# Attention, experts and a squared-ReLU layer on one core: the units of a step in another order

## The chip, the cores and the metric

One core of one Trainium2 chip runs the whole program in one launch. The metric is the device time in microseconds (us); before the change it is 1945.49 us, the median of 3 runs (1945.02 to 1945.93).

## The reference

Three parts follow one another; everything is float32.

```python
# 1. attention: 4 batches, 8 heads, 576 positions, head size 64
scores = q @ k.T / 8        # heads 0-3: the last 32 positions
                            # heads 4-7: every 4th of the last 128
x = softmax(scores) @ v     # -> x [2304, 512]
# 2. experts: 8 experts of width 1024, all of them for every token
P = exp(x @ w_gate - max)   # then 8 rounds that scale rows and columns
out = sum_e P[:, e] * (relu(x @ w1[e]) @ w2[e])
# 3. a dense layer of width 2048
y = relu(out @ w_in) ** 2 @ w_out
```

## The kernel before, in words

After the attention the kernel runs 80 steps. Steps 0 to 31 take the 8 experts in quarters of 256 hidden columns for tokens 0 to 1023 (and a single block of 256 tokens, 1024 to 1279); steps 32 to 63 (32 is `NS1`) take the same weights for tokens 1280 to 2303; steps 64 to 71 and 72 to 79 are the dense layer for the two pairs of token blocks. `first` holds 0, 32, 64, 72; `TURN` is 4, `SCALED` 3.

Every float32 number is split into a high part, rounded to the type that TensorE multiplies, and a low part, and a product is three: high by high, high by low, low by high. Each layer multiplies 2 x 2 blocks with seven products in place of eight (Winograd's form), so the operands are sums and differences of blocks, and results are built up in PSUM banks, copied to another bank as a common part, and added to.

In layer one the seven units of step i are u1 to u7 (`l1_pair`), six products of 512 columns each, 1.36 us. They use three banks, tiles s, pt, xt: bank_a (u1, u3), bank_b (a copy of u1's result, then u4, u5, u6) and bank_c (u2, u7). After u4 ScalarE copies bank_b to s2 (L771), after u5 to s3 (L775); VectorE adds bank_c to s3 (L776), and only then may u7 overwrite bank_c; after u7 it adds bank_c to s2 (L787). L723 takes the ReLU of a result times the token's gate as r1 (u3), r2 (u5), r3 (u6), r4 (u7).

Layer two of step i - 1 runs in step i, where a step is "mixed" (5 to 64 and 73 to 79). Its units are v1m to v7m for output half m = 0, 1 (`l2_mixed`, line 946), three products each, 0.68 us: a half unit. Their left operands are made from r1 to r4: GpSimd forms the differences (L736, "mix", and L734, r3 - r5), ScalarE casts the high part (L702), VectorE subtracts the low part (L705). Operand 11 comes from u3, 22 from u5, 21 from u6, t1 to t4 from the mix after u7. v1 uses 11, v2 uses 21, v3 22, v4 t4, v5 t1, v6 t2, v7 t3. Each chain of units shares banks: v6, v3 and then v7, v4 add to one bank that VectorE (L957) has to read in between; half 0 ends its chain in bank x, half 1 in bank z, so v41 may write z only after the add of v71 has read it. "cp" is a ScalarE copy into half 1's second bank; that bank is bank_a, so cp waits until L723 has read r1 from it. In steps 0 to 31 there are also us (layer one of the single block, 24 products of 256 columns, L806), w0 and w1 (its layer two, six products each, L849), and the weights of the next step are split: a high part on ScalarE (L174) and a low part on VectorE (L178), with sums of blocks on GpSimd (L192 to L197, L246 to L251). In steps 32 to 63 the split weights are fetched from DRAM.

The order is written by hand. `names` lists a mixed step's units; a + joins units into one slot. `run` issues a unit and then what is due in its slot; `after(k, f)` puts f into the k-th slot from now. Every engine works through its own instructions in the order issued, and the SyncE queue (SP) issues all transfers in order. So the list sets both TensorE's order and, by the counts k, that of the other four. In a step of 5 to 30 the list has 17 slots; the parts of the next weights fall in fixed slots (`prep_w`).

Other work rides along: `split_on` splits activation blocks for later steps (a cast, then a low part, two stores and a GpSimd subtraction), and `narrow_on` turns int64 words of the dense layer's weights (they hold float64) into float32 in pieces of three VectorE stages each; `work` gives the slots of the stages, `loads` those of a piece's load. Three pieces (`DEEP`) were done in steps 3 and 4, the rest from step 33. `turn` (line 916) transposes the single block's sums in step 32.

Of the kernel before, what the change touches and what calls it, by code (L numbers as in the profile page):

```python
# [36 lines left out]
NS1 = E * SPE  # L37
# [14 lines left out]
def tile_kernel(ctx: ExitStack, tc: tile.TileContext, a):  # L52
# [113 lines left out]
    def prep_w(i, layers=(1, 2)):  # L166
# [63 lines left out]
        elif i >= 0:  # L230
# [22 lines left out]
            if SCALED <= i < NS1:  # L253
                at = (7, 8, 9, 9, 16, 17) if i == NS1 - 1 else (7, 8, 9, 9, 14, 16) if i > TURN else (7, 8, 9, 9, 13, 15)
            elif moe:
                at = (0, 0, 0, 1, 9, 11) if i == 0 else (8, 10, 11, 12, 16, 17) if i == 1 else (1, 3, 6, 7, 13, 15)
            else:
                at = (11, 13, 14, 14, 20, 22) if late else (14, 15, 16, 16, 21, 22) if n == first[2] + 2 else (12, 13, 14, 14, 19, 20)
# [25 lines left out]
    def load_raw():  # L284

        n = asked[0]
        if n == len(raw_pieces):
            return
        asked[0] += 1
        which, s, k = raw_pieces[n]  # L290
        z = deep[0] if n < DEEP else (raw2, acc[1])[n % 2] if n < MID else apart[0]
        src = loaded[n] = z.bitcast(I32).rearrange("p (n w) -> p n w", w=2)
        nc.sync.dma_start(
            src.rearrange("p n w -> p (n w)"),
            a["w_in" if which == 0 else "w_out"][s].bitcast(I32)[:, 2 * NP * k:2 * NP * k + 2 * NP],
        )

    def narrow(n):
# [5 lines left out]
        if n < DEEP:  # L304
            topf = deep[1][:, half]
        elif n < MID:
            topf = sums.rearrange("p b c -> p (b c)")[:, half]
        else:
            topf = apart[1]
# [373 lines left out]
    def l1_pair(i):  # L683
# [24 lines left out]
        def out_mixed(fc, t, src, k):  # L708
# [23 lines left out]
            elif (fc, t) == (1, 0):  # L732
                operand("21", g, 2, 3)
                after(4, lambda: nc.gpsimd.tensor_tensor(out=r3, in0=r3, in1=r5, op=ALU.subtract))  # L734
            else:
# [95 lines left out]
    def l2_units(i, which):  # L831
# [85 lines left out]
        def turn(ch, c, src):  # L917

            ps = single_bank()
            turned(ps, src.rearrange("p (k n) -> p k n", n=128))  # L920
            y = raw1.rearrange("p b c -> p (b c)")[:, 512 * c:512 * c + 512]
            nc.scalar.copy(y, ps)
            nc.sync.dma_start(
                y_dram[:, :, ch * 128:ch * 128 + 128], y.rearrange("p (k n) -> p k n", k=KC)
            )
# [84 lines left out]
    with tc.manual_schedule():  # L1010
# [212 lines left out]
        for i in range(len(steps) + 1):  # L1223
# [23 lines left out]
            if mixed(i - 1):  # L1247
# [3 lines left out]
                if i == first[2]:  # L1251
                    names = "v10 u1 v20 us v50+v60 v51+v30 v70 u2 v11 u3 v40 u4+cp v21+v61 u5 v71+v31 u6 v41 u7"
                elif i == NS1:
                    u |= zip(("w0", "w1"), l2s)
                    names = "v10 u1 v20 w0 v50+v60 w1 v51+v30 u2 v11 u3 v70 u4+cp v21+v61 u5 v40+v71+v31 u7 v41 u6"
                elif i == first[1] - 1:
                    names = "u1 v10 u2 v20 w0 u3 v11 u4 v50+v60+cp u5 v51+v30+v70 u7 v21+v61 u6 w1 v40+v71+v31 us v41"
                elif i == first[2] - 1:
                    names = "u1 v10+v11 u2 v20 u3 u4 v50+v60+cp u5 v51+v30+v70 u7 v21+v61 u6 v71+v40+v31 v41"
                elif i == len(steps) - 1:  # L1260
                    names = "u1 v10+v11 u2 v20 u3 u4 v50+v60+cp u5 v51+v30+v70 u6 v21+v61 u7 v71+v40+v31 v41"
                elif i < NS1:
                    names = "u1 v10 u2 v20 w0 u3 v50+v60+v11 u4+cp v51+v30+v70 u5 v21+v61 u7 w1 v40+v71+v31 u6 v41 us"
                else:
                    names = "u1 v10+v11 u2 v20 u3 v50+v60 u4+cp v51+v30+v70 u5 v21+v61 u7 v40+v71+v31 u6 v41"

# [5 lines left out]
            elif i == TURN:  # L1272
                order = l2[:5] + l2s + l1[:4] + [u for k, n in ((5, 4), (6, 6), (7, 5)) for u in (l2[k], l1[n])]
                l2, l2s = [], []
            else:
                for u in (l1[4], l1[6], l1[5]) if i == first[3] else l1[4:]:
                    order += l2[:1] + [u]
                    l2 = l2[1:]
# [17 lines left out]
            if i == 2 * NS1 - 1:  # L1296
                apart[:] = xb(), post[0].tile([128, T], F32, tag="pp", name="pp", bufs=3)
            if i in (SCALED - 1, SCALED):
                deep.append(xb())
# [6 lines left out]
            if TURN + 2 <= i < TURN + 18:  # L1306
                split_on(0, 8, 9)
            elif NS1 + 4 <= i < 2 * NS1 - 4:
# [10 lines left out]
            elif SCALED <= i <= TURN:  # L1319
                work = (1, 4, 7) if i == SCALED else (1, 4, 7, 13, 15, 17)  # L1320
            elif NS1 <= i < 2 * NS1 - 3:
                work = () if i == NS1 else (4, 8) if NS1 + 4 <= i < NS1 + 20 else (4, 6, 8)
                loads = (15, 17) if i == NS1 else ()
            elif 2 * NS1 - 1 <= i < first[3] - 1 and done[0] < len(raw_pieces):
                work = () if i == 2 * NS1 - 1 else (2, 4, 6)
                loads = (8,)
            for k, u in enumerate(order):
# [4 lines left out]
                if k in work and done[0] < end:  # L1332
                    narrow_on()
                    if not begun and asked[0] < end and i < 2 * NS1 - 1:
                        load_raw()
# [89 lines left out]
```

## Time and profile before

| | before |
|---|---|
| profiled execution's own time | 1945.29 us |
| its span | 1943.5 us |
| TensorE products (PE) | 1888.3 us busy, 97% |
| VectorE (DVE) | 1651.7 us, 85% |
| ScalarE (ACT) | 925.2 us, 48% |
| GpSimd (POOL) | 755.1 us, 39% |
| mean granted TensorE clock | 0.998 |

Line numbers are those of the kernel before. The page's first part gives each engine's busy time; the waits name the instruction that waited and the one that released it; the timeline lists instructions in order of time, with the idle time before one in brackets; a stretch's row gives busy times of the engines in it. In names, xt, pt, s and mm are PSUM banks. u1 and u3 write s from blk, u4, u5 write pt from sum, u6 pt from blk, u2 and u7 xt from sum.

### The profile page before, as it was taken

The page shows a single profiled execution, that of the slowest core. Times are in us where ns is not written, and L with a number is a line of the kernel's source. Part 1 is how long each engine was busy: PE and PEld are TensorE (multiplying, and loading weights), DVE is VectorE, ACT ScalarE, POOL GpSimd, SP SyncE. Part 2 cuts the span into 40 slices and gives each one's busy share as a digit, 9 for nine tenths or more (in the row PEclk, how much of TensorE's full clock was granted, in tenths as well). Part 3 has the DMA queues.
Part 4 walks back from the last instruction along what each step waited for, and adds up shares of the span by engine and source line. Part 5 has one row for each costly group of instructions (what it writes and reads, how often), then busy time and mean ns, then how long its engine had stood idle before and what let it go on. Part 6 is the DMA issues. An engine that isn't in the chain of part 4 may idle for free.

```text
span 1943.5 us, 28331 instructions
## 1 busy us (share of the span) xinstructions
PE 1888.3 (97%) x10247; PEld 1539.0 (79%) x10247; DVE 1651.7 (85%) x2344; ACT 925.2 (48%) x1568; POOL 755.1 (39%) x648
## 2 busy tenths in 40 slices
PE   8999899999999999999999999999999999999998
PEld 6778788878887888887777787777878888887887
DVE  6787889999999989887799999999999898875676
ACT  6754445444545444444434444443434466553444
POOL 3532356555655555553223233332222334421221
PEclk9999999999999999999999999999999999999999
DMA  8684576657667665557977768676767798889462
GB/s 301 220 310 177 202 243 219 218 226 249 232 222 248 219 223 199 203 216 292 367 257 273 270 254 311 248 293 235 278 246 265 288 352 305 289 313 379 176 247 76
DMA packets 166204, 492.76 MB, mean 254 GB/s; under 512 B 16992, under 2 KB 36336, under 8 KB 166064
## 3 DMA queue, kind: packets, MB, share of 16 engines
q1 hardware_dynamic: 166064, 490.96, 68.7%
q8 instruction: 80, 1.31, 0.3%
q14 instruction: 60, 0.49, 0.1%
HBM read 282.15 MB, written 208.74 MB: 253 GB/s over the span
## 4 chain that ended last, share of the span: by engine, by line
PE 64%; DVE 26%; issue 4%; ACT 3%; DMA 2%; POOL 0%; SPq 0%; DVEq 0%; ACTq 0%; POOLq 0%
PE mm L849 11%; PE xt L625 10%; PE pt L625 9%; PE mm L946 9%; PE s L625 8%; PE s L946 8%; DVE acc L957 6%; DVE g L705 5%; PE mm L806 3%; DVE s L776 2%; DVE mixl L178 2%; PE xt L946 2%; DVE suml L178 2%; DVE mix L723 1%; DVE blkl L178 1%
## 5 line engine op out<-in xcount | busy, mean ns | idle before, releaser
L736 POOL TENSOR_TENSOR r<-mix,r 128x512 f32<-128x512 f32 x67 | 86.8, 1295 | 605.6 <-DVE mix L723 605.6
L705 DVE TENSOR_TENSOR g<-r,g 128x512 fp32r<-128x512 f32 x268 | 253.3, 964 | 25.1 <-ACT g L702 23.8
L702 ACT CAST g<-r 128x512 fp32r<-128x512 f32 x268 | 165.3, 621 | 113.5 <-DVE acc L957 52.8
L946 PE MATMUL mm<-g,w2h 128*128 128x512 f32 x670 | 208.1, 391 | 7.8 <-DVE g L705 5.4
L946 PE MATMUL s<-g,mixh 128*128 128x512 f32 x670 | 206.9, 390 | 0.0
L705 DVE TENSOR_TENSOR g<-mix,g 128x512 fp32r<-128x512 f32 x201 | 190.9, 950 | 3.0 <-ACT g L702 3.0
L957 DVE TENSOR_TENSOR acc<-s,acc 128x512 f32<-128x512 f32 x260 | 172.8, 684 | 11.3 <-PE s L946 11.2
L957 DVE TENSOR_TENSOR acc<-mm,acc 128x512 f32<-128x512 f32 x260 | 177.3, 682 | 0.2 <-PE mm L946 0.2
L702 ACT CAST g<-mix 128x512 fp32r<-128x512 f32 x201 | 124.5, 620 | 107.8 <-DVE mix L723 58.6
L946 PEld LDWEIGHTS mm<-g,w2h 128*128 128x128 f32 x670 | 125.6, 188 | 37.1 <-DVE g L705 6.9
L625 PE MATMUL xt<-x_hi,sumh 128*128 128x512 f32 x316 | 130.9, 414 | 18.7 <-DVE s L776 17.7
L946 PEld LDWEIGHTS s<-g,mixh 128*128 128x128 f32 x670 | 126.0, 188 | 26.7 <-ACT mm L968 0.4
L246 POOL TENSOR_TENSOR raw<-raw 128x256 f32<-128x256 f32 x36 | 38.2, 1060 | 273.6 <-DVE w2l L178 249.2
L734 POOL TENSOR_TENSOR mix<-mix,r 128x512 f32<-128x512 f32 x67 | 103.0, 1538 | 95.7 <-DVE g L705 95.7
L946 PE MATMUL mm<-g,w2l 128*128 128x512 f32 x335 | 130.4, 389 | 0.0
L849 PE MATMUL mm<-w2h,g 128*128 128x512 f32 x416 | 129.7, 393 | 0.1
L625 PE MATMUL s<-x_hi,blkh 128*128 128x512 f32 x316 | 124.1, 393 | 0.0
L625 PE MATMUL s<-x_lo,blkh 128*128 128x512 f32 x316 | 124.0, 392 | 0.0
L625 PE MATMUL xt<-x_lo,sumh 128*128 128x512 f32 x316 | 123.6, 391 | 0.0
L625 PE MATMUL xt<-x_hi,suml 128*128 128x512 f32 x316 | 123.6, 391 | 0.0
L625 PE MATMUL s<-x_hi,blkl 128*128 128x512 f32 x316 | 123.6, 391 | 0.0
L625 PE MATMUL pt<-x_hi,sumh 128*128 128x512 f32 x316 | 123.1, 389 | 0.0
(269 smaller groups left out, 4956.3 us busy)
## 6 DMA issues: line engine op xcount, KB each, us to landing
raw<-in_w SPq DMA_DIRECT2D x61, 512.0 KB, 4.2
w_blkh<-blkh SPq DMA_DIRECT2D x40, 512.0 KB, 5.1
w_blkl<-blkl SPq DMA_DIRECT2D x40, 512.0 KB, 5.9
w_sumh<-sumh SPq DMA_DIRECT2D x40, 512.0 KB, 4.1
w_suml<-suml SPq DMA_DIRECT2D x40, 512.0 KB, 2.8
w_w2h<-w2h SPq DMA_DIRECT2D x40, 512.0 KB, 5.8
w_w2l<-w2l SPq DMA_DIRECT2D x40, 512.0 KB, 5.8
blkh<-w_blkh SPq DMA_DIRECT2D x40, 512.0 KB, 3.7
```

What stands on the lines that cost most here:

```text
L178: nc.vector.tensor_tensor(out=w[1], in0=src, in1=w[0].bitcast(F32), op=ALU.subtract)
L246: tt(out=r[:, 1, 1], in0=r[:, 0, 1], in1=r[:, 1, 1], op=ALU.add)
L625: nc.tensor.matmul(ps, w[:, c], z[:, x, j], start=start and k == 0, stop=stop and k == 5, skip_group_check=True)
L702: after(k, lambda: nc.scalar.copy(b[:, 0], src))
L705: lambda: nc.vector.tensor_tensor(out=b[:, 1], in0=src, in1=b[:, 0].bitcast(F32), op=ALU.subtract),
L734: after(4, lambda: nc.gpsimd.tensor_tensor(out=r3, in0=r3, in1=r5, op=ALU.subtract))
L736: sub = lambda o, x, y: nc.gpsimd.tensor_tensor(out=o, in0=x, in1=y, op=ALU.subtract)
L776: after(1, lambda: nc.vector.tensor_tensor(out=made["s3"], in0=bank_c, in1=made["s3"], op=ALU.add))
L806: nc.tensor.matmul(ps, w[:, c], z[:, kc], start=k == 0, stop=k == len(terms) - 1)
L849: nc.tensor.matmul(ps, g[:, c0 * 128:c0 * 128 + 128], wt[:, fc], start=k == 0, stop=k == 3 * FC - 1)
L946: nc.tensor.matmul(ps, w[wt][:, c], block[n][:, g], start=start and k == 0, stop=stop and k == 2, skip_group_check=True)
L957: nc.vector.tensor_tensor(out=o, in0=ps, in1=o, op=ALU.add)
```

## The change

The lists of unit names change. In steps 5 to 30 v60 goes behind u4 (with v51), v30 and v70 behind u5, so that u5 comes ahead of them and there are two half units between u4 and u5 and four between u5 and u7; the list grows to 18 slots. Steps 33 to 62 and 73 to 78 change alike (14 to 15 slots). In most lists v71 is issued before v40. Steps 31, 32, 63, 64 and 79 get lists of their own kind: u7 behind v21 and v61, u6 before v41 in step 32, us before v20 in step 64, w0 before v20 in step 32, v70 beside v71 in step 79. Steps 4 and 72 issue u5, u6, u7 in this order in place of u5, u7, u6, and there the subtraction r3 - r5 comes 6 slots behind u6, not 4. `turn` uses u2's bank. The mix operands of steps 5 to 30 are split one slot later. The split blocks of steps 6 to 21 are cast in slot 5 and finished in slot 6. The third narrowed piece moves from step 4 to steps 22 (load) and 23 to 25 (one stage each), with two more buffers; in the last stretch of steps 33 to 35 and 52 to 60 the third stage goes from slot 8 to slot 9.

```diff
--- before.py
+++ after.py
@@ -251,7 +251,7 @@
                 tt(out=r[:, 1, 0], in0=r[:, 1, 0], in1=r[:, 0, 0], op=ALU.subtract)
 
             if SCALED <= i < NS1:
-                at = (7, 8, 9, 9, 16, 17) if i == NS1 - 1 else (7, 8, 9, 9, 14, 16) if i > TURN else (7, 8, 9, 9, 13, 15)
+                at = (7, 8, 9, 9, 16, 17) if i == NS1 - 1 else (7, 8, 9, 9, 15, 17) if i > TURN else (7, 8, 9, 9, 13, 15)
             elif moe:
                 at = (0, 0, 0, 1, 9, 11) if i == 0 else (8, 10, 11, 12, 16, 17) if i == 1 else (1, 3, 6, 7, 13, 15)
             else:
@@ -288,7 +288,7 @@
             return
         asked[0] += 1
         which, s, k = raw_pieces[n]
-        z = deep[0] if n < DEEP else (raw2, acc[1])[n % 2] if n < MID else apart[0]
+        z = deep[-1 if n == DEEP - 1 else 0] if n < DEEP else (raw2, acc[1])[n % 2] if n < MID else apart[0]
         src = loaded[n] = z.bitcast(I32).rearrange("p (n w) -> p n w", w=2)
         nc.sync.dma_start(
             src.rearrange("p n w -> p (n w)"),
@@ -302,7 +302,7 @@
         low, high = src[:, :, 0], src[:, :, 1]
         half = slice(NP * (n % 2), NP * (n % 2) + NP)
         if n < DEEP:
-            topf = deep[1][:, half]
+            topf = deep[-1 if n == DEEP - 1 else 1][:, half]
         elif n < MID:
             topf = sums.rearrange("p b c -> p (b c)")[:, half]
         else:
@@ -731,7 +731,7 @@
                 operand("22", g, *((7, 8) if i + 1 in first else (6, 7)))
             elif (fc, t) == (1, 0):
                 operand("21", g, 2, 3)
-                after(4, lambda: nc.gpsimd.tensor_tensor(out=r3, in0=r3, in1=r5, op=ALU.subtract))
+                after(6 if i in (TURN, first[3]) else 4, lambda: nc.gpsimd.tensor_tensor(out=r3, in0=r3, in1=r5, op=ALU.subtract))
             else:
                 sub = lambda o, x, y: nc.gpsimd.tensor_tensor(out=o, in0=x, in1=y, op=ALU.subtract)
 
@@ -916,7 +916,7 @@
 
         def turn(ch, c, src):
 
-            ps = single_bank()
+            ps = own[NS1][2] if spare else bank("mm")
             turned(ps, src.rearrange("p (k n) -> p k n", n=128))
             y = raw1.rearrange("p b c -> p (b c)")[:, 512 * c:512 * c + 512]
             nc.scalar.copy(y, ps)
@@ -1249,20 +1249,20 @@
                 u = dict(zip(("u1", "u2", "u3", "u4", "u5", "u6", "u7"), l1))
                 u |= zip(("us", "w0", "w1"), l1s + l2s)
                 if i == first[2]:
-                    names = "v10 u1 v20 us v50+v60 v51+v30 v70 u2 v11 u3 v40 u4+cp v21+v61 u5 v71+v31 u6 v41 u7"
+                    names = "v10 u1 us v20 v50+v60 v51+v30 v70 u2 v11 u3 v40 u4+cp v21+v61 u5 v71+v31 u6 v41 u7"
                 elif i == NS1:
                     u |= zip(("w0", "w1"), l2s)
-                    names = "v10 u1 v20 w0 v50+v60 w1 v51+v30 u2 v11 u3 v70 u4+cp v21+v61 u5 v40+v71+v31 u7 v41 u6"
+                    names = "v10 u1 w0 v20 v50+v60 w1 v51+v30 u2 v11 u3 v70 u4+cp v21+v61 u5 v71+v40+v31 u7 u6 v41"
                 elif i == first[1] - 1:
-                    names = "u1 v10 u2 v20 w0 u3 v11 u4 v50+v60+cp u5 v51+v30+v70 u7 v21+v61 u6 w1 v40+v71+v31 us v41"
+                    names = "u1 v10 u2 v20 w0 u3 v11 u4 v50+v60+cp u5 v51+v30+v70 v21+v61 u7 w1 v71+v40+v31 u6 us v41"
                 elif i == first[2] - 1:
-                    names = "u1 v10+v11 u2 v20 u3 u4 v50+v60+cp u5 v51+v30+v70 u7 v21+v61 u6 v71+v40+v31 v41"
+                    names = "u1 v10+v11 u2 v20 u3 u4 v50+v60+cp u5 v51+v30+v70 v21+v61 u7 v71 u6 v40+v31 v41"
                 elif i == len(steps) - 1:
-                    names = "u1 v10+v11 u2 v20 u3 u4 v50+v60+cp u5 v51+v30+v70 u6 v21+v61 u7 v71+v40+v31 v41"
+                    names = "u1 v10+v11 u2 v20 u3 u4 v50+v60+cp u5 v51+v30 u6 v21+v61 v70+v71 u7 v40+v31 v41"
                 elif i < NS1:
-                    names = "u1 v10 u2 v20 w0 u3 v50+v60+v11 u4+cp v51+v30+v70 u5 v21+v61 u7 w1 v40+v71+v31 u6 v41 us"
+                    names = "u1 v10 u2 v20 w0 u3 v50+v11 u4+cp v60+v51 u5 v30+v70 v21+v61 u7 w1 v71+v40+v31 u6 v41 us"
                 else:
-                    names = "u1 v10+v11 u2 v20 u3 v50+v60 u4+cp v51+v30+v70 u5 v21+v61 u7 v40+v71+v31 u6 v41"
+                    names = "u1 v10+v11 u2 v20 u3 v50 u4+cp v60+v51 u5 v30+v70 v21+v61 u7 v71+v40+v31 u6 v41"
 
                 def together(fs):
                     return lambda: [f() for f in fs]
@@ -1270,10 +1270,10 @@
                 order = [together([(u | v)[n] for n in item.split("+")]) for item in names.split()]
                 l2, l2s, l1s, ahead = [], [], [], []
             elif i == TURN:
-                order = l2[:5] + l2s + l1[:4] + [u for k, n in ((5, 4), (6, 6), (7, 5)) for u in (l2[k], l1[n])]
+                order = l2[:5] + l2s + l1[:4] + [u for k in range(3) for u in (l2[5 + k], l1[4 + k])]
                 l2, l2s = [], []
             else:
-                for u in (l1[4], l1[6], l1[5]) if i == first[3] else l1[4:]:
+                for u in l1[4:]:
                     order += l2[:1] + [u]
                     l2 = l2[1:]
             order += l2 + l2s + l1s
@@ -1295,7 +1295,7 @@
                 splits.append(blocks_of(1, y_dram[:, :, :2 * T], y0 + raw))
             if i == 2 * NS1 - 1:
                 apart[:] = xb(), post[0].tile([128, T], F32, tag="pp", name="pp", bufs=3)
-            if i in (SCALED - 1, SCALED):
+            if i in (SCALED - 1, SCALED, TURN + 18, TURN + 19):
                 deep.append(xb())
             if i == TURN + 2:
                 y = two(xb()) + two(xb())
@@ -1304,7 +1304,7 @@
                 y1 = two(mix32) + tuple(post[0].tile([128, T], F32, tag="pp", name="pp", bufs=3) for _ in range(2))
                 splits.append(blocks_of(2, y_dram[:, :, PAIRS[1]:], y1 + two(mixes[0][0]) + two(xb().bitcast(F32R))))
             if TURN + 2 <= i < TURN + 18:
-                split_on(0, 8, 9)
+                split_on(0, 5, 6)
             elif NS1 + 4 <= i < 2 * NS1 - 4:
                 split_on(1, 5, 9)
             elif 2 * NS1 < i < 2 * NS1 + 7:
@@ -1317,9 +1317,11 @@
             if i == SCALED - 1:
                 loads = (3,)
             elif SCALED <= i <= TURN:
-                work = (1, 4, 7) if i == SCALED else (1, 4, 7, 13, 15, 17)
+                work = (1, 4, 7)
+            elif TURN + 18 <= i < NS1 - 2:
+                work, loads = ((), (10,)) if i == TURN + 18 else ((6,), ())
             elif NS1 <= i < 2 * NS1 - 3:
-                work = () if i == NS1 else (4, 8) if NS1 + 4 <= i < NS1 + 20 else (4, 6, 8)
+                work = () if i == NS1 else (4, 8) if NS1 + 4 <= i < NS1 + 20 else (4, 6, 9)
                 loads = (15, 17) if i == NS1 else ()
             elif 2 * NS1 - 1 <= i < first[3] - 1 and done[0] < len(raw_pieces):
                 work = () if i == 2 * NS1 - 1 else (2, 4, 6)
@@ -1331,7 +1333,7 @@
                 end = DEEP if i < NS1 else MID if i < 2 * NS1 - 1 else len(raw_pieces)
                 if k in work and done[0] < end:
                     narrow_on()
-                    if not begun and asked[0] < end and i < 2 * NS1 - 1:
+                    if not begun and asked[0] < (end if i >= NS1 else DEEP - 1) and i < 2 * NS1 - 1:
                         load_raw()
                 if k in loads:
                     load_raw()
```

## Rows read from the trace of the kernel before

**Rows 1.** The page, part 1: busy time and share of the span by engine.
```profile
PE 1888.3 (97%) x10247; PEld 1539.0 (79%) x10247; DVE 1651.7 (85%) x2344; ACT 925.2 (48%) x1568; POOL 755.1 (39%) x648
```

**Rows 2.** Waits of TensorE: total us, times, longest us.
```profile
PE xt L625 <- DVE s L776: 17.7, 43, 1.4
PE s L946 <- DVE acc L957: 10.7, 27, 0.8
PE mm L946 <- DVE g L705: 5.4, 3, 3.0
```

**Rows 3.** The chain in order of time: start, us, what; two unbroken runs.
```profile
656.37 2.80 PE mm L806 x24
...
1592.06 9.52 PE mm L849 x42
```

**Rows 4.** Busy time by stretch: PE, PEld, DVE, ACT, POOL, granted clock, DMA, GB/s.
```profile
223.90:227.60 3.70, 3.70 (x11) 2.90 (x10) 2.61 (x4) 0.00 (x0) 0.97 (x1) 0.54 0.00 0
246.86:889.50 642.64, 629.44 (x3002) 516.82 (x3001) 583.15 (x715) 312.35 (x489) 355.21 (x308) 1.00 0.63 224
...
947.90:951.10 3.20, 3.20 (x9) 2.48 (x8) 2.36 (x4) 0.00 (x0) 0.09 (x1) 0.52 1.02 416
963.11:1535.41 572.30, 561.21 (x2438) 454.95 (x2436) 523.71 (x771) 240.18 (x424) 172.45 (x125) 1.00 0.71 266
...
1359.79:1379.35 19.56, 19.33 (x85) 15.69 (x84) 18.63 (x29) 7.95 (x14) 5.56 (x5) 1.00 0.67 256
...
1807.01:1904.00 96.99, 96.76 (x421) 78.46 (x420) 72.11 (x104) 44.13 (x82) 27.43 (x21) 1.00 0.57 217
```

**Rows 5.** Timeline of TensorE, one step: u7 and v41 wait, v40 starts.
```profile
622.17 0.39 PE L946 MATMUL s<-g,mixl 128*128 128x512 f32 x1
622.81 0.50 PE L625 MATMUL xt<-x_hi,sumh 128*128 128x512 f32 x1 [0.25 <-DVE s L776]
...
625.66 0.62 PE L946 MATMUL mm<-g,w2h 128*128 128x512 f32 x2
...
629.60 0.73 PE L946 MATMUL s<-g,w2h 128*128 128x512 f32 x2 [0.38 <-DVE acc L957]
```

**Rows 6.** Timeline of VectorE from w1's add to r1.
```profile
625.86 0.75 DVE L875 SCALAR_TENSOR_TENSOR acc<-mm,ptile,acc 128x512 f32<-128x512 f32 x1 [0.67 <-PE mm L849]
626.53 1.22 DVE L178 TENSOR_TENSOR suml<-sums,sumh 128x1024 fp32r<-128x1024 f32 x1
...
634.55 1.22 DVE L705 TENSOR_TENSOR g<-mix,g 128x512 fp32r<-128x512 f32 x1
...
640.10 0.67 DVE L705 TENSOR_TENSOR g<-mix,g 128x512 fp32r<-128x512 f32 x1
...
641.83 0.68 DVE L723 SCALAR_TENSOR_TENSOR r<-s,pp 128x512 f32<-128x512 f32 x1
```

**Rows 7.** Timeline of ScalarE: the copy L771.
```profile
644.55 0.59 ACT L771 COPY s<-pt 128x512 f32<-128x512 f32 x1
```

**Rows 8.** Timeline of GpSimd beside operand 21's low part.
```profile
634.04 1.18 POOL L193 TENSOR_TENSOR sums<-raw 128x256 f32<-128x256 f32 x1
```

**Rows 9.** Timeline of TensorE, steps 4 and 5: u7 and v20.
```profile
207.92 0.50 PE L625 MATMUL xt<-x_hi,sumh 128*128 128x512 f32 x1 [1.44 <-DVE s L776]
...
222.65 0.50 PE L946 MATMUL mm<-g,w2h 128*128 128x512 f32 x1 [2.96 <-DVE g L705]
```

**Rows 10.** Timeline of TensorE, steps 32 and 33: w1 and v20.
```profile
922.28 0.73 PE L849 MATMUL mm<-w2h,sg 128*128 128x512 f32 x2 [1.24 <-ACT raw L922]
...
944.42 0.50 PE L946 MATMUL mm<-g,w2h 128*128 128x512 f32 x1 [0.97 <-ACT g L702]
...
946.30 0.50 PE L946 MATMUL mm<-g,w2h 128*128 128x512 f32 x1 [1.38 <-DVE g L705]
```

**Rows 11.** Timeline of TensorE, steps 72 and 73: u7 and v20.
```profile
1781.58 0.50 PE L625 MATMUL xt<-x_hi,sumh 128*128 128x512 f32 x1 [1.38 <-DVE s L776]
...
1791.80 0.50 PE L946 MATMUL mm<-g,w2h 128*128 128x512 f32 x1 [1.07 <-DVE g L705]
```

## The prediction

> **What bounds the kernel now.** I read the busy times first: TensorE works 1888.3 of the 1943.5 us span [rows 1], so at most some 55 us of plain idle time can go, plus what a restart costs. The sum of waits of TensorE then says where: the largest item is the first product of u7 (it overwrites bank_c) waiting 43 times for the add L776 that reads bank_c, the second a unit v41 waiting 27 times for an accumulation L957, the third three long waits for an operand's low part L705 [rows 2]. Third comes the unhindered speed, from long unbroken runs in the chain: 42 products of 512 columns take 9.52 us, 0.2267 each, and one us unit takes 2.80 us [rows 3]. A step in 6 to 30 issues 96 products of 512 columns and one us: 96 x 0.2267 + 2.80 = 24.56 us. It takes 642.64 / 25 = 25.71 [rows 4]. A step in 34 to 62 issues 84: 19.04 us; it takes 572.30 / 29 = 19.73 [rows 4]. These two stages lose 28.7 and 20.1 us.
>
> The timeline prices a wait. A product's record is 0.39 us long though the next may start 0.227 after it, so a wait costs its idle time plus 0.16, and the first interval afterwards is 0.11 longer. In one step u7 loses 622.81 - 622.17 - 0.23 = 0.41 and v41 0.38 + 0.16 = 0.54, with two restarts 1.17 us [rows 5]: the 1.15 lost per step.
>
> I make the sum against the profiled execution's own 1945.29 us (span 1943.5 and 1.8 around it); the median of the runs shown is 1945.49, so the two agree.
>
> **Steps 6 to 30 (25 steps).** What goes: u5 now has v30, v70, v21 and v61 between it and u7, 2.72 us in place of 1.36. The copy L775 and the add L776 need 0.2 + 0.59 + 0.68, and L776 stands ahead of the adds of v30 and v70 in VectorE's queue, so u7's wait goes. v71 is issued before v40, its add comes one add (0.60) sooner, and v41's 0.54 goes.
>
> What comes: only v60 and v51 (1.36 us) now stand between u4 and u5, where three half units (2.04) stood, and u5 must not write bank_b before the copy L771 has read it. L771 is the fourth in ScalarE's queue: cp, the w2 cast, the cast of operand 11, L771. cp waits for r1 (L723). From the end of r1 to the end of L771 the rows give 645.14 - 642.51 = 2.63 us [rows 6, 7]. r1 in turn ends a chain in which VectorE never rests: from w1's add (625.86) to r1's end (642.51) is 16.65 us [rows 6]. Let W be the end of w1 on TensorE (625.66, where v40 starts [rows 5]); r1 then ends at W + 16.85. In the new order suml (1.13, slot 12) falls ahead of u7's add and leaves this chain, and r3 then waits some 0.33 for u6: W + 16.05. GpSimd's mix starts 1.1 us sooner against this chain, so operand 21's low part overlaps it less: up to 0.4 more, W + 15.6. It can't be less: the add of w0 waits for w0's end (W + 12.5), and behind it stand 0.66 + 0.60 + 1.13 + 0.68. So u5 starts at W + 18.3 to 18.75, while TensorE is there at W + 17.76 (24.56 less the 6.80 from u5 to the end of w1). The step becomes 18.3 + 6.80 + 0.13 = 25.25 to 25.7. In steps 6 to 21 the split block's cast and rest move from slots 8, 9 to 5, 6, into VectorE's rest before the w2 low part, but the GpSimd subtraction behind them now meets that low part: up to 0.3 more; on SP their two stores now stand ahead of those of the w2 parts, for which nothing in the step waits. I take 25.4, **8 us** gained; bounds 13 us and, at 26.0, a loss of 7. The mix operand's move (14, 16 to 15, 17) follows the longer slot list and is kept in the chain above; a piece's stage in slot 6 of steps 23 to 25 (1.1 to 1.8 us) fills the same rest of VectorE and I price it at nothing; its load in step 22 has nothing waiting behind it on SP but that step's last stores. Without that cover it is 4 us in all.
>
> What VectorE pays beside GpSimd is the open price. Operand 21's low part, two inputs in SBUF, took 1.22 us while GpSimd ran L193, the same kind 0.67 in quiet [rows 6, 8]. The Trainium skill (GPSIMD Engine Reference, section Key points) says that GpSimd shares its SBUF interfaces with VectorE and contends with instructions of two SBUF inputs. By that rule alone every such instruction beside GpSimd keeps its doubled price, the step is 25.7 and the whole sum 1909; by the timeline, where the contended piece ends about 0.55 behind GpSimd's instruction, it is the sum below.
>
> **Steps 34 to 62 (29).** The only wait is u7's. The new order again puts 2.72 us between u5 and u7, and what stood before L776 in VectorE's queue (adds of v30 and v70, in three-stage steps one narrowing stage, slot 8 to 9) moves behind it. I followed the queue through a step: r1 ends about 6.9 us after u1's start, a stage 8.7, operands t4 and 11 9.9, a second stage 10.9, a split rest 11.5 at the latest; L776 starts at 11.7 behind L775 and u7 at 13.6, a slack of 1.2. u5 does not wait here: no weight cast stands before L771, which ends 0.5 us ahead of it. VectorE is busy 18.63 us in the fullest step [rows 4], below 19.04. I take 19.1 us a step: 29 x 0.63, **18 us**; bounds 20 and, if VectorE's queue holds steps at 19.4, 9.
>
> **Steps 4 and 5.** u7 waits 1.44 idle and v20 of step 5 2.96 [rows 9], for work that the third narrowed piece pushed back on VectorE; after it TensorE runs at a granted clock of 0.54 for 3.70 us [rows 4], near its lower level of 1.2 GHz. Now the piece is gone from here, u6 goes before u7, so operand 21 is ready a unit and a us sooner. 1.44 + 0.27, 2.96 + 0.27, 3.70 x 0.46 = 1.7, and 0.7 of step 5's two usual waits: 7.3, taken as **7**; bounds 4 and 8. r3 - r5 is moved from 4 to 6 slots because u7's mix now comes later; t4 needs it only at v40, so it costs nothing.
>
> **Steps 31 to 33.** The turn's copy holds spare's bank and w1 waits 1.24; v20 of step 33 waits 0.97 and 1.38 [rows 10], again with a stretch at 0.52 behind it (3.20 us, 1.5 lost) [rows 4]. u6 before v41 puts operand 21 first in both queues, some 2 us sooner. Removed: 1.4 + 1.1 + 1.6 + 1.5, and 0.7 where w0 covers v20 of step 32. Added: the turn's transposes stand only v20 (0.68) behind w0 and wait 0.3 for its add, and u2 must wait for the last turn's copy out of its own bank, 0.2 + 0.59 [rows 7] + 0.2. Net **5**; bounds 1 and 6.
>
> **The rest.** Steps 72, 73: u7's 1.38 + 0.27 and v20's 1.07 + 0.27 [rows 11], by the same move as in step 4: **3** (1 to 3.4). Steps 73 to 78: 96.99 / 5 = 19.40 [rows 4] to 19.06, **2** (0 to 2). Step 79: v41's 0.8, the longest of its kind [rows 2], with v71 two units ahead: **1** (0 to 2). Steps 63, 64: nothing (1 either way).
>
> Sum: 8 + 18 + 7 + 5 + 3 + 2 + 1 = 44; 1945.3 - 44 = **1901 us**.
>
> **Rivals.** *u5's wait eats steps 6 to 30*: the doubled prices hold, steps stay at 25.7; sum 36, 1909 us. For: VectorE is busy 583 of 643 us there [rows 4]. Against: suml does leave the chain.
> *VectorE's queue takes u7's place in steps 34 to 62*: total VectorE work of 18.63 leaves 0.4 a step, so L776 or v31's add, which u1 needs, is late; steps at 19.4, sum 35, 1910 us. For: that margin. Against: 1.2 us of slack at u7. Both rivals together: 1918.
> *Slower*: r1 comes so late that u5 pays more than all else gives. All other terms are 36 us, so each of 25 steps must grow by 1.45 to 27.2 us, which is r1 ending after W + 17.6; at W + 18.0 steps take 27.6 and the time is 1956. For: all of ScalarE's four instructions hang on that one event. Against: the chain ends at W + 16.85 today and loses an instruction of 1.13.
> *It doesn't do what it says*: waits move to the next unit with the same length because the same adds end last; only steps 4, 5 and 33 change little, 1943 us. Against: in steps 34 to 62 nothing else is late by the timeline.
>
> **How the numbers follow.** As summed 0.62 (1891 to 1911); u5 0.13; VectorE's queue 0.10; both 0.06; not as it says 0.04; slower 0.05. A measurement here can tell 0.2 per cent, 3.9 us, from no change. Faster 0.91, same 0.04, slower 0.05. The range reaches from the better bounds, some 1889, over both rivals together to 1921.
>
> **What would show it.** In the changed profile: u7 <- L776 nearly gone from TensorE's waits; a new item, u5 (pt, L625) <- ACT s L771, some 25 times 0.3 to 0.8 us; steps of 25.4 in 6 to 30 and 19.1 in 34 to 62; no granted clock near 0.5 around steps 5 and 33. I am wrong if u5 waits over 1 us in each step, or if steps 34 to 62 stay above 19.4.

## The result and the profile after

The changed kernel takes 1913.63 us (median of 4 runs, 1910.39 to 1915.29); the kernel before took 1945.26 on the same chip (4 runs, 1942.1 to 1945.93). The ratio is 0.9839, 95% interval 0.9821 to 0.9856: 31.6 us less, where 44 were forecast. The profiled execution took 1915.29 us, its span is 1913.5, which is 30.0 less than before.

The page shows the first surprise: VectorE runs the same 2344 instructions in 50 us less [rows 1].

```profile
PE 1875.1 (98%) x10247; PEld 1543.8 (81%) x10247; DVE 1601.4 (84%) x2344; ACT 926.3 (48%) x1568; POOL 763.3 (40%) x648
```

TensorE's waits (total us, times, longest us) are the list to set beside [rows 2]:

```profile
PE pt L625 <- ACT s L771: 13.1, 28, 1.1
...
PE s L946 <- ACT mm L968: 3.0, 1, 3.0
...
PE xt L491 <- issue: 2.2, 1, 2.2
...
PE xt L625 <- ACT raw L922: 0.7, 1, 0.7
...
PE xt L909 <- DVE acc L875: 0.5, 1, 0.5
PE s L625 <- DVE acc L957: 0.5, 2, 0.2
...
PE xt L625 <- DVE s L776: 0.3, 1, 0.3
```

u7's wait for L776 fell from 17.7 us to 0.3, v41's 27 waits are gone, and the named new one is there: u5 for L771. The second item, one wait of 3.0 for L968, was in no step of the forecast.

Busy time by stretch, columns as in [rows 4]: steps 6 to 30, steps 34 to 62, step 64, and 3.4 us inside step 64.

```profile
246.88:882.38 635.50, 624.51 (x3002) 518.56 (x3001) 540.49 (x722) 309.67 (x489) 363.46 (x308) 1.00 0.64 227
...
952.45:1507.13 554.68, 554.15 (x2438) 456.12 (x2436) 520.78 (x771) 242.96 (x423) 171.62 (x125) 1.00 0.74 274
1526.98:1553.76 26.78, 23.42 (x107) 18.93 (x105) 24.16 (x32) 14.47 (x26) 10.44 (x10) 0.94 0.80 292
...
1537.10:1540.50 3.40, 3.33 (x8) 2.66 (x9) 3.24 (x6) 2.02 (x4) 0.00 (x0) 0.51 0.96 381
```

In steps 34 to 62 TensorE is busy 554.15 of 554.68 us. At the prediction's 19.04 a step it would be 552.2; of the 2.5 us left, 1.6 lie in steps 34 and 35. From the start of u1 in one step to that in another, in the two profiled executions, and in that of the last kernel of the experiments:

| stretch | before | after | forecast | measured | last kernel |
|---|---|---|---|---|---|
| start to step 4 | 196.32 | 201.44 | 0 | +5.1 | 196.56 |
| steps 4, 5 | 50.54 | 45.44 | -7 | -5.1 | 44.48 |
| steps 6 to 30 | 642.64 | 635.50 | -8 | -7.1 | 616.96 |
| steps 31 to 33 | 73.61 | 70.07 | -5 | -3.5 | 68.47 |
| steps 34 to 62 | 572.30 | 554.68 | -18 | -17.6 | 554.67 |
| steps 63, 64 | 42.89 | 46.63 | 0 | +3.7 | 42.98 |
| steps 72, 73 | 36.49 | 33.02 | -3 | -3.5 | 33.06 |
| steps 74 to 78 | 96.99 | 95.39 | -2 | -1.6 | 95.31 |
| step 79 to the end | 39.50 | 39.13 | -1 | -0.4 | 39.10 |

Steps 65 to 71, whose order does not change, take 192.2 us before and after and 192.7 in the last kernel.

One step of the new steady state, first VectorE, then ScalarE, then u5 on TensorE:

```profile
711.28 0.68 DVE L705 TENSOR_TENSOR g<-mix,g 128x512 fp32r<-128x512 f32 x1
711.88 1.22 DVE L178 TENSOR_TENSOR blkl<-raw,blkh 128x1024 fp32r<-128x1024 f32 x1
713.02 0.68 DVE L723 SCALAR_TENSOR_TENSOR r<-s,pp 128x512 f32<-128x512 f32 x1
```
```profile
713.79 0.57 ACT L1001 COPY s<-mm 128x512 f32<-128x512 f32 x1 [3.48 <-DVE r L723]
714.27 1.06 ACT L174 CAST w2h<-raw 128x1024 fp32r<-128x1024 f32 x1
715.22 0.62 ACT L702 CAST g<-r 128x512 fp32r<-128x512 f32 x1
715.74 0.58 ACT L771 COPY s<-pt 128x512 f32<-128x512 f32 x1
```
```profile
698.03 0.62 PE L946 MATMUL s<-g,mixh 128*128 128x512 f32 x2
...
711.55 0.39 PE L625 MATMUL s<-x_hi,blkl 128*128 128x512 f32 x1
...
716.38 0.50 PE L625 MATMUL pt<-x_hi,sumh 128*128 128x512 f32 x1 [0.36 <-ACT s L771]
```

w1 ended at W = 698.03. r1 ends at 713.70, W + 15.67 (forecast W + 15.6 to 16.05), L771 2.62 later (2.63), u5 starts at W + 18.35 (18.3 to 18.75), and the step takes 25.3. But the reader also sees what the forecast read as a given: the last product that r1 needs begins at 711.55, yet the low part blkl, issued a little earlier, stands ahead of r1 for 1.14 us; and behind r1 the w2 cast, 0.95, stands ahead of L771. Both are choices of the order.

### The profile page after: what moved, and what is told of

The parts are those of the page before. It is cut to its first block, busy times and chain, and to the rows that moved or that the text cites. A ratio compares the mean times of both kernels' runs of the same rounds, so it can differ in the third digit from the quotient of the medians.

```text
span 1913.5 us, 28261 instructions
## 1 busy us (share of the span) xinstructions
PE 1875.1 (98%) x10247; PEld 1543.8 (81%) x10247; DVE 1601.4 (84%) x2344; ACT 926.3 (48%) x1568; POOL 763.3 (40%) x648
## 4 chain that ended last, share of the span: by engine, by line
PE 84%; DVE 7%; ACT 4%; issue 3%; POOL 0%; DMA 0%; DVEq 0%; ACTq 0%; POOLq 0%
PE pt L625 15%; PE mm L946 14%; PE s L946 12%; PE mm L849 12%; PE xt L625 11%; PE s L625 9%; PE mm L806 5%; DVE g L705 2%; ACT w2h L174 1%; PE xt L946 1%; DVE r L723 1%; DVE acc L957 1%; PE xt L491 1%; ACT g L702 1%; PE s L448 1%
## 5 line engine op out<-in xcount | busy, mean ns | idle before, releaser
L705 DVE TENSOR_TENSOR g<-r,g 128x512 fp32r<-128x512 f32 x268 | 222.6, 841 | 32.1 <-ACT g L702 31.1
L957 DVE TENSOR_TENSOR acc<-mm,acc 128x512 f32<-128x512 f32 x260 | 177.2, 681 | 3.4 <-PE mm L946 2.8
L957 DVE TENSOR_TENSOR acc<-s,acc 128x512 f32<-128x512 f32 x260 | 177.0, 681 | 0.7 <-PE s L946 0.6
L946 PEld LDWEIGHTS mm<-g,w2h 128*128 128x128 f32 x670 | 125.7, 188 | 26.1
L734 POOL TENSOR_TENSOR mix<-mix,r 128x512 f32<-128x512 f32 x67 | 114.3, 1707 | 74.0 <-DVE g L705 74.0
L625 PE MATMUL xt<-x_hi,sumh 128*128 128x512 f32 x316 | 123.9, 392 | 1.0 <-ACT raw L922 0.7
L625 PE MATMUL pt<-x_lo,sumh 128*128 128x512 f32 x316 | 123.3, 390 | 0.0
L625 PE MATMUL pt<-x_hi,suml 128*128 128x512 f32 x316 | 123.3, 390 | 0.0
```

The source lines that it names most:

```text
L625: nc.tensor.matmul(ps, w[:, c], z[:, x, j], start=start and k == 0, stop=stop and k == 5, skip_group_check=True)
L705: lambda: nc.vector.tensor_tensor(out=b[:, 1], in0=src, in1=b[:, 0].bitcast(F32), op=ALU.subtract),
L734: after(6 if i in (TURN, first[3]) else 4, lambda: nc.gpsimd.tensor_tensor(out=r3, in0=r3, in1=r5, op=ALU.subtract))
L946: nc.tensor.matmul(ps, w[wt][:, c], block[n][:, g], start=start and k == 0, stop=stop and k == 2, skip_group_check=True)
L957: nc.vector.tensor_tensor(out=o, in0=ps, in1=o, op=ALU.add)
```

## The experiments

Theory: in steps 6 to 30 one chain, r1, cp, w2 cast, L771, sets u5, and its length is a matter of the order in two queues. Rival: VectorE's work beside GpSimd sets the step, whatever the order.

**Block part behind r1** (changed kernel, steps 5 to 30):
```diff
-(2, 5, 10, 12) if TURN + 1 < n < NS1
+(2, 6, 10, 12) if TURN + 1 < n < NS1
```


> The changed kernel with one edit: in steps 5 to 30 the low part of the next step's blk weights (L178 blkl, 1.22 us on VectorE) is issued one slot later, behind r1 in VectorE's queue instead of ahead of it. Theory (a chain from r1 over ScalarE's queue to L771 sets u5): r1 ends about 1.1 us sooner, L771 with it, u5's wait of 0.36 to 0.8 is gone in all 25 steps, they take 24.6 to 24.8 us in place of 25.28 to 25.8, and the time falls by 15 to 19 us to about 1896. Rival (VectorE's sum of work beside GpSimd sets the step, whatever its order): what is saved ahead of r1 is paid again by a later low part, a wait of the same size shows at u5 or u7, steps stay above 25.2 and the time is within 4 us of the changed kernel's.

1896.26 us (1896.02 to 1896.64), ratio to before 0.9745 (0.9730 to 0.9759). Steps take 24.82 to 24.93. VectorE of this kernel, one step:

```profile
671.38 0.69 DVE L723 SCALAR_TENSOR_TENSOR r<-s,pp 128x512 f32<-128x512 f32 x1
671.99 1.22 DVE L178 TENSOR_TENSOR blkl<-raw,blkh 128x1024 fp32r<-128x1024 f32 x1
```

**w2 cast behind L771** (changed kernel, steps 5 to 30):
```diff
-(7, 8, 9, 9, 15, 17) if i > TURN
+(8, 9, 9, 9, 15, 17) if i > TURN
```


> The changed kernel with one edit: in steps 5 to 30 the cast of the w2 weights (L174 w2h, 1.05 us on ScalarE) and its low part are issued one slot later, so that the copy L771 is ahead of the cast in ScalarE's queue. r1 itself is not touched. Theory (ScalarE's queue between r1 and L771 sets u5): r1 ends where it does now, L771 ends 0.9 to 1.0 us sooner, u5's wait is gone, steps take 24.6 to 24.9 us and the time falls by 13 to 19 us to about 1897. Rival (VectorE's late r1 alone matters, or the w2 low part that now comes later holds the next unit): u5 still waits, or a wait of the same size comes at u7 (L776) or a later half unit; steps stay above 25.2, time within 4 us of the changed kernel's.

1895.28 us (1894.21 to 1896.91), ratio 0.9740 (0.9726 to 0.9755). blkl still stands ahead of r1, L771 follows one cast after it, and u5 starts unhindered; steps take 24.68, four of them 25.1. ScalarE of this kernel:

```profile
673.94 0.57 ACT L1001 COPY s<-mm 128x512 f32<-128x512 f32 x1 [3.48 <-DVE r L723]
674.42 0.63 ACT L702 CAST g<-r 128x512 fp32r<-128x512 f32 x1
674.94 0.59 ACT L771 COPY s<-pt 128x512 f32<-128x512 f32 x1
...
676.00 1.05 ACT L174 CAST w2h<-raw 128x1024 fp32r<-128x1024 f32 x1
```

Either edit alone takes the wait away, at two different places of one chain. The rival is out: VectorE does the same work in both (busy 542.5 and 539.9 us in steps 6 to 30, 540.5 in the changed kernel).

**Step 64's swap undone** (changed kernel):
```diff
-v10 u1 us v20 v50+v60
+v10 u1 v20 us v50+v60
```


> The changed kernel with step 64's order of v20 and the us unit put back as before the change. Theory (the swap alone put the copy L968 of operand 60 behind VectorE's narrowing stage): the wait of 2.98 us at v30 of step 64 and the half-clock stretch behind it go, step 64 takes 23.1 us in place of 26.8, the time falls by 3 to 4 us. Rival (the wait comes from the units of step 63, which now end otherwise): step 64 keeps 26 us or more and the time stays.

1909.44 us (1907.88 to 1912.01); step 64 takes 23.72 in place of 26.78, the wait for L968 is gone. The 0.6 us above the 23.1 expected is a wait of v20 for an operand's low part:

```profile
1529.64 0.50 PE L946 MATMUL mm<-g,w2h 128*128 128x512 f32 x1 [1.19 <-DVE g L705]
```

It is gone, and step 64 takes 23.13, where the list of step 63 is undone too (the run of both edits below): that list cost the 0.6.

**The list of steps 33 to 62 and 73 to 78 alone** (kernel before; the list of the diff, and (4, 6, 9)):
```diff
-"... u3 v50+v60 u4+cp v51+v30+v70 u5 v21+v61 u7 v40+v71+v31 u6 v41"
+"... u3 v50 u4+cp v60+v51 u5 v30+v70 v21+v61 u7 v71+v40+v31 u6 v41"
```


> The kernel before with only the new order of steps 33 to 62 and 73 to 78 (and the third narrowing stage in slot 9). Theory (u7's wait in those steps was a matter of the distance between u5 and u7 alone, independent of the other parts): steps 34 to 62 take 19.04 to 19.15 us, steps 73 to 78 some 19.08, the time falls by 17 to 20 us to 1925 to 1928; steps 6 to 30 stay at 25.6 to 25.8. Rival (the stages help each other, over the state in which the first stage leaves the narrowed pieces): less than 14 us.

1926.56 us (1924.26 to 1927.83), ratio 0.990 (0.9883 to 0.9916). Steps 34 to 62 take 555.10 us, as in the changed kernel, steps 74 to 78 95.34, steps 6 to 30 stay at 643.24. So the new list, with the third stage in slot 9, does it without the other parts. What in the list counts was not taken apart: it puts more units between u5 and u7, and it also moves adds behind L776 in VectorE's queue.

**The list of steps 5 to 30 alone** (kernel before):
```diff
-"... u3 v50+v60+v11 u4+cp v51+v30+v70 u5 v21+v61 u7 w1 v40+v71+v31 u6 v41 us"
+"... u3 v50+v11 u4+cp v60+v51 u5 v30+v70 v21+v61 u7 w1 v71+v40+v31 u6 v41 us"
-(7, 8, 9, 9, 14, 16) if i > TURN
+(7, 8, 9, 9, 15, 17) if i > TURN
```


> The kernel before with only the new order of steps 5 to 30 (and the mix operand in slots 15 and 17 of its longer list); the split blocks stay in slots 8 and 9 and the third narrowed piece where it was. Theory (the list alone replaces the two old waits of 1.15 us by one wait of u5 for L771): steps 6 to 30 take 25.3 to 25.4 us throughout, the time falls by 7 to 10 us to about 1938. Rival (the list pays only with the split blocks moved to slots 5 and 6, out of the way of the w2 low part): steps 6 to 21 stay at 25.6 or more and the time falls by 4 us or less.

1934.73 us (1933.22 to 1935.57), ratio 0.9936 (0.9923 to 0.9950). All of steps 6 to 30 take 25.30 to 25.34, 632.88 in sum. The time fell by more than the 7 to 10 us expected: in step 33, which this edit does not touch, v20's two waits are there as before (0.96 and 1.37), but no half clock follows them in this run, and the step takes 22.29 in place of 23.90. The sum of steps 6 to 30 is 2.6 us less than with the whole change, so something else in it costs; the split blocks' move to slots 5 and 6 is the candidate. First GpSimd, then VectorE of the changed kernel, in a step of 25.8:

```profile
303.29 1.29 POOL L354 TENSOR_TENSOR xb<-xb 128x512 f32<-128x512 f32 x1
```
```profile
303.96 1.17 DVE L705 TENSOR_TENSOR g<-mix,g 128x512 fp32r<-128x512 f32 x1
305.05 1.21 DVE L178 TENSOR_TENSOR blkl<-raw,blkh 128x1024 fp32r<-128x1024 f32 x1
306.19 0.68 DVE L723 SCALAR_TENSOR_TENSOR r<-s,pp 128x512 f32<-128x512 f32 x1
```

The split's subtraction L354 runs beside an operand's low part ahead of r1, which takes 1.17 in place of 0.68, and r1 is that much later.

**The third piece, with step 4's order** (kernel before; the diff's lines for deep, work, asked and TURN's order, and 6 for 4 slots). In this kernel step 72 takes operand t4 ahead of the subtraction r3 - r5, with the same instructions.
```diff
-work = (1, 4, 7) if i == SCALED else (1, 4, 7, 13, 15, 17)
+work = (1, 4, 7)
...
-[u for k, n in ((5, 4), (6, 6), (7, 5)) for u in (l2[k], l1[n])]
+[u for k in range(3) for u in (l2[5 + k], l1[4 + k])]
```


> The kernel before with only the third narrowed piece moved from steps 3 and 4 to steps 22 to 29, and u6 ahead of u7 in step 4. Theory (the piece on VectorE caused u7's wait of 1.44 and v20's of 2.96 and the half clock behind them): the stretch from u1 of step 4 to u1 of step 6 falls from 50.5 to 45 or 46 us, steps 23 to 25 stay within 0.2 us, the time falls by 4 to 6 us. Rival (the waits of step 5 come from the order of its own units): the stretch stays above 48.5 us.

1940.77 us (1938.96 to 1941.91), ratio 0.9967 (0.9955 to 0.9980). Steps 4 and 5 take 45.64 us, steps 23 to 25 stay within 0.1. The piece and the order of u6 and u7 were not tried apart.

**Both edits, lists of steps 63 and 64 undone** (changed kernel; the first two edits above, 8 for 7 in step 31 too, and):
```diff
-v10 u1 us v20 v50+v60
+v10 u1 v20 us v50+v60
-v51+v30+v70 v21+v61 u7 v71 u6 v40+v31 v41
+v51+v30+v70 u7 v21+v61 u6 v71+v40+v31 v41
```


> The changed kernel with both earlier edits (blk low part behind r1, w2 cast behind L771, in step 31 too) and with the lists of steps 63 and 64 as before the change. Theory (the two edits act on one chain, r1 to L771; either removes u5's wait, so they do not add beyond what TensorE needs): steps 6 to 30 all take 24.66 to 24.72 us, also those that took 25.1 with the cast edit alone and 24.86 with the block edit alone; step 5 takes 26.1 us; steps 63 and 64 take 19.8 and 23.1 us; together 1886 to 1890 us. Rival (VectorE's sum of work sets the step once both are in): steps stay at 24.86 and the time is 1891 or more.

1889.55 us (1888.1 to 1891.48). Steps 6 to 30 all take 24.66 to 24.68; the four slow ones are gone. Together the edits save 18.7 us of the changed kernel's 635.50, alone 13.9 and 16.9: they don't add, since TensorE is then the bound (busy 616.83 of 616.83 us). Step 64 takes 23.13; step 5 takes 26.56 where 26.1 was expected, step 63 20.03 where 19.8 was.

**Step 64's narrowing stage one slot later** (changed kernel with both edits):
```diff
-work = () if i == 2 * NS1 - 1 else (2, 4, 6)
+work = () if i == 2 * NS1 - 1 else (3, 4, 6) if i == 2 * NS1 else (2, 4, 6)
```


> The changed kernel with both edits in steps 5 to 30; step 64 keeps the us unit ahead of v20, but its first narrowing stage (L313, L317 on VectorE) is issued in slot 3, behind the add of v20, in place of slot 2. Theory (the wait of v30 in step 64 is the narrowing stage ahead of v20's add in VectorE's queue): the wait of 2.98 us falls below 1.2, no half clock follows, step 64 takes 23.2 to 24.2 us. Rival (the operands' low parts beside GpSimd hold that add, the stage is innocent): step 64 stays above 25.5 us.

1889.56 us (1888.59 to 1892.97); step 64 takes 23.69 with the swap kept. VectorE and TensorE in step 64, first of the changed kernel:

```profile
1533.78 0.95 DVE L313 TENSOR_SCALAR pp<-xb 128x512 int32<-128x512 int32 x1
1534.76 1.10 DVE L317 SCALAR_TENSOR_TENSOR pp<-xb,pp 128x512 int32<-128x512 int32 x1
1535.78 0.68 DVE L957 TENSOR_TENSOR acc<-mm,acc 128x512 f32<-128x512 f32 x1
```
```profile
1537.17 1.22 PE L946 MATMUL s<-g,mixh 128*128 128x512 f32 x2 [2.98 <-ACT mm L968]
```

then of this kernel:

```profile
1510.23 0.68 DVE L957 TENSOR_TENSOR acc<-mm,acc 128x512 f32<-128x512 f32 x1
1510.83 0.41 DVE L313 TENSOR_SCALAR pp<-xb 128x512 int32<-128x512 int32 x1
1511.27 1.10 DVE L317 SCALAR_TENSOR_TENSOR pp<-xb,pp 128x512 int32<-128x512 int32 x1
```
```profile
1511.62 0.73 PE L946 MATMUL s<-g,mixh 128*128 128x512 f32 x2 [0.99 <-ACT mm L968]
```

v20 moved from slot 2 to slot 3, the narrowing stage stayed in slot 2, so v20's add fell behind 2 us of it. With the stage behind the add the wait is 0.99.

**Split blocks and the turn's bank undone** (changed kernel):
```diff
-split_on(0, 5, 6)
+split_on(0, 8, 9)
-ps = own[NS1][2] if spare else bank("mm")
+ps = single_bank()
```


> The changed kernel with two edits in stretches that do not touch: the split blocks of steps 6 to 21 back in slots 8 and 9, and the turn's transposes (L909) back in the bank that the singles use. Split blocks: theory (at slots 5 and 6 GpSimd's subtraction L354 runs beside an operand's low part ahead of r1 and costs more than it saves) all of steps 6 to 21 take 25.3 us, the stretch from step 6 to 31 falls from 635.5 to 632 or 633 us; rival (the move pays, as it was priced before) those steps rise to 25.6 or more. Bank: theory (the own bank takes away w1's wait and adds u2's wait and one of the transposes) step 32 takes 24.2 to 24.5 us in place of 23.75, with w1 waiting for L922 about 1.2 us again; rival (the new waits cost as much as the old) step 32 stays within 0.2 of 23.75.

1907.40 us (1907.22 to 1908.27), ratio 0.9797 (0.9781 to 0.9814). Steps 6 to 30 take 633.39: the split's move cost 2.1 us. Step 32 takes 22.80 in place of 23.75, and both theories of the bank missed: w1's wait does not come back. TensorE of this kernel in step 32, the turn's transposes and then w1:

```profile
906.00 0.66 PE L909 MATMUL mm<-ident,acc 128*128 128x128 f32 x4 [0.54 <-DVE acc L875]
...
907.88 0.62 PE L849 MATMUL mm<-w2h,sg 128*128 128x512 f32 x2
```

With w0 ahead of v20 the transposes follow v20, no longer v50 and v60, so their copy L922 runs beside v50 and v60 and w1 starts unhindered in the old bank. What the bank of its own brings is u2's wait of 0.68 for L922 in the changed kernel.

**All that helped** (the two edits, the stage in slot 3, step 63's list undone; and in step 33 operand t3's low part behind r1):
```diff
-((4, 5), (5, 6), (6, 7), (8, 9)) if i >= NS1
+((4, 5), (5, 6), (6, 8 if i == NS1 else 7), (8, 9)) if i >= NS1
```


> The changed kernel with the blk low part behind r1, the w2 cast behind L771 in steps 5 to 30, step 64's first narrowing stage in slot 3, step 63's list as before the change, and in step 33 the low part of operand t3 one slot later, behind r1. Theory: steps 6 to 30 take 24.67 us, step 64 takes 23.4 to 23.8 us; in step 33 r1 ends 0.6 us sooner, u5's wait of 1.14 for L771 falls to about 0.5 and the step from 21.0 to 20.4 us; the time is 1886 to 1890 us. Rival for step 33 (the low parts beside GpSimd are the delay, not their order against r1): it stays at 21.0 us.

1888.45 us (1887.43 to 1889.07). Step 33 takes 20.40; step 64 takes 23.12, below the 23.4 to 23.8 expected (with step 63's new list it took 23.69). TensorE at u5 of step 33, first of the changed kernel, then of this one:

```profile
942.79 0.50 PE L625 MATMUL pt<-x_hi,sumh 128*128 128x512 f32 x1 [1.14 <-ACT s L771]
```
```profile
918.11 0.50 PE L625 MATMUL pt<-x_hi,sumh 128*128 128x512 f32 x1 [0.54 <-ACT s L771]
```

VectorE shows what remains: three low parts beside GpSimd, 1.43 each, then r1.

```profile
911.47 4.28 DVE L705 TENSOR_TENSOR g<-r,g 128x512 fp32r<-128x512 f32 x3 [0.82 <-ACT g L702]
915.67 0.68 DVE L723 SCALAR_TENSOR_TENSOR r<-s,pp 128x512 f32<-128x512 f32 x1
```

**The same, turn's bank undone:**
```diff
-ps = own[NS1][2] if spare else bank("mm")
+ps = single_bank()
```


> The kernel of the run before this one (all edits that helped), with the turn's transposes back in the bank that the singles use. Theory (w0 ahead of v20 already frees that bank for w1; the bank of its own only makes u2 wait for the copy L922): step 32 takes 22.8 us in place of 23.75, no wait for L922 is left on TensorE, steps 33 and 64 stay at 20.4 and 23.1 us, the time is 1884 to 1889 us. Rival (the 22.8 seen with the split blocks moved back owed something to these): step 32 stays above 23.4 us.

1886.11 us (1885.48 to 1886.76), ratio to before 0.9691 (0.9677 to 0.9704). Step 32 takes 22.77. This beats both kernels, the changed one by 27.5 us (1913.63 less 1886.11).

## Why the prediction was right, and where it was off

The sum was 12.6 us too low: 31.6 us were gained, not 44. The measured 1913.63 lies in the stated range (1889 to 1921), but just outside the band of the sum itself (1891 to 1911) and next to the 1909 and 1910 of two rivals. Neither rival happened, so that nearness is chance. The two largest terms came by the mechanism that was named; the gap lies elsewhere.

**Steps 34 to 62**: right in place and size, 17.6 of 18, and shown by the list without the other parts. The rival in which VectorE's queue holds these steps fell as a whole: 19.04 us in most steps, 19.13 or 19.14 in steps 53 to 60 with their three narrowing stages, no wait of u7. In steps 34 and 35, which have three stages too, it happened in small: they take 19.75 and 19.91 (19.97 and 19.80 before), and the u1 behind each waits for an add L957, as that rival had it (the two waits of 0.2 in the list of waits after the change).

**Steps 6 to 30**: right; 25.42 on average against 25.4. The rival of the doubled prices fell, and its premise with it: VectorE's busy time there went from 583.15 [rows 4] to 540.49 in place of staying. The groups of VectorE in steps 6 to 30 (count, busy, mean ns) show where, first before, then after:

```profile
L705 DVE TENSOR_TENSOR g<-r,g 128x512 fp32r<-128x512 f32 x100 | 113.2, 1151 | 0.0
...
L178 DVE TENSOR_TENSOR mixl<-raw,mixh 128x1024 fp32r<-128x1024 f32 x26 | 57.7, 2220 | 0.0
```
```profile
L705 DVE TENSOR_TENSOR g<-r,g 128x512 fp32r<-128x512 f32 x100 | 73.5, 735 | 20.6 <-ACT g L702 20.6
...
L178 DVE TENSOR_TENSOR mixl<-raw,mixh 128x1024 fp32r<-128x1024 f32 x26 | 44.6, 1714 | 0.0
```

The same 100 low parts cost 40 us less: their mean is now near the quiet kind's 0.67, where before it was near the 1.22 of the one beside GpSimd [rows 6, 8]. They have not left GpSimd's side: before and after, all 100 overlap one of its instructions by 0.4 us or more. What changed is which of the two starts first. Before, 75 of them began while a GpSimd instruction had over 0.5 us to run; each ended 0.55 us behind that instruction and took 1.22 to 1.47. After, 75 begin ahead of GpSimd's instruction or within 0.2 us of the end of one and take 0.67 to 0.71; the other 25 begin some 0.3 us before its end and take 0.85 to 0.88. Now GpSimd pays: L734, ahead of which a low part now begins (0.04 us in the step below), takes 1.79 on average in place of 1.30, and GpSimd's busy time in steps 6 to 30 rises from 355.21 [rows 4] to 363.46. GpSimd and VectorE in one step, first before, then after:

```profile
610.12 1.30 POOL L734 TENSOR_TENSOR mix<-mix,r 128x512 f32<-128x512 f32 x1 [0.69 <-DVE g L705]
...
610.50 2.62 DVE L705 TENSOR_TENSOR g<-r,g 128x512 fp32r<-128x512 f32 x2
```
```profile
605.59 0.68 DVE L705 TENSOR_TENSOR g<-r,g 128x512 fp32r<-128x512 f32 x1
...
605.63 1.79 POOL L734 TENSOR_TENSOR mix<-mix,r 128x512 f32<-128x512 f32 x1
```

This is read from the traces; no run changes the start of such a pair alone. The rule of the Trainium skill (GPSIMD Engine Reference, section Key points), that the two engines contend where VectorE reads two inputs from SBUF, agrees with these pairs and with the low part of 1.17 beside L354 (0.68 alone); it does not say which of the two pays. One choice inside this term was not weighed: the split blocks' move was priced at up to 0.3 us a step and kept; it cost 2.1 in all. And the term's better bound, 13 us, does not follow from its floor of 25.25 us a step, which gives 11.

**Steps 63, 64, "nothing (1 either way)"**: this step failed, by 3.7 us: 3.1 from the swap of us and v20 (26.78 against 23.72 with it undone) and 0.6 from step 63's list. I priced both on TensorE alone and did not follow the fixed slots: the narrowing stage keeps its slot number when the list is reordered. The wait of 2.98 was followed by products 0.43 us apart, at a granted clock of 0.51, the lower level of 1.2 GHz; over 3.40 us that is 1.7 of the loss. That part need not have come: in the run with the split blocks and the turn's bank undone, the same wait (3.00) was followed by full clock, and step 64 took 25.33.

**Steps 4, 5**: 5.1 of 7. The cause was right as far as it was tried (the piece with step 4's order gives 4.9). The rest is in short waits: in step 5 u5 waits 0.60 for L771, with blkl ahead of r1 there too, and half units wait 0.35 and 0.42 for low parts. The block edit takes off another 1.0 to 1.5 in the five runs that have it.

**Steps 31 to 33**: 3.5 of 5. v20's waits and the half clock went as forecast. The 1.5 us for that clock were not sure to be there, though: the run of the list of steps 5 to 30 alone had the same waits without it. u2's wait for L922 (0.68) came as forecast. Not seen were u5's 1.14 in step 33, of which 0.6 was t3's low part ahead of r1, and that the bank edit bought nothing: it cost 0.95.

**The start**: 5.1 us of the gap are not of the change. In the thirteen profiled executions, all with the same code up to step 1, u1 of step 1 starts between 98.23 and 103.80; the changed kernel's is the latest. In four of them TensorE ran at half clock for some 3 to 10 us before 54 us, and there u1 starts at 100.86 to 103.80; in the other nine, without such a stretch, at 98.23 to 100.04. The small terms (72 to 79) were within 0.6 each; what the prediction calls steps 73 to 78 are the five steps 74 to 78. In sum, against the profiled 1915.3: 5.1 + 3.7 + 1.9 + 1.5 + 0.9 + 0.4 + 0.5 for the small ones = 14.0 of the 14.3 us by which 1901 was too low.

Why early waits in the first 100 us differ between executions of one code (the wait of xt L491 is marked "issue") stays open. So does the rest of the wait in step 33: the low parts were not moved away from GpSimd.

## What to carry to other kernels

When a list of work is reordered, follow what is pinned to slot numbers, not only what is in the list: a stage, a cast or a low part that keeps its number lands ahead of something that it used to follow. When a wait is moved rather than removed, walk back its chain queue by queue and ask at each step which instruction ahead has no need to be there: here 1 us in either of two queues was worth 14 to 17 us over 25 steps. A bank or buffer added together with a new order should be tried without it.

## What the runs showed of the hardware

A wait in the first stage was followed by a stretch of half clock too. TensorE of the changed kernel, and the stretch behind its wait by busy time (columns as in [rows 4]); the kernel before ran the same 10 us at a granted 1.00.

```profile
24.92 0.69 PE L491 MATMUL xt<-pts,v 128*64 128x64 f32 x8 [2.23 <-issue]
```
```profile
24.00:34.00 10.00, 9.08 (x158) 7.17 (x159) 3.15 (x9) 5.17 (x11) 1.65 (x2) 0.54 0.70 221
```

A granted clock near 0.5, the 1.2 GHz level, followed idle times of 2.23, 2.98 and 2.96 [rows 9], and also 0.97 and 1.38 close together [rows 10]; behind 1.14 in step 33 of the changed kernel there was none. The length of the wait alone does not decide it. TensorE behind the wait in step 64 in the run with the split blocks and the turn's bank undone, which has the changed kernel's lists there:

```profile
1530.82 0.74 PE L946 MATMUL s<-g,mixh 128*128 128x512 f32 x2 [3.00 <-ACT mm L968]
```
```profile
1530.82:1534.22 3.40, 3.40 (x15) 2.79 (x16) 3.24 (x6) 1.95 (x3) 0.00 (x0) 1.00 0.95 386
```

The granted clock stayed at 1.00 behind 3.00 us; in the changed kernel it fell to 0.51 behind 2.98. It also stayed at 1.00 behind 0.96 and 1.37 in step 33 in the run of the list of steps 5 to 30 alone. What else decides it, these traces do not show.

In these traces VectorE's low parts (two inputs in SBUF) and GpSimd's instructions hold each other up, and the one that starts later pays: a low part that begins beside a running GpSimd instruction ended 0.55 us behind it, and one that begins first took its 0.68 while GpSimd's L734 took 1.79 in place of 1.30.
